# Sixteen heads of attention and a feed-forward: written out in one straight program, or as one loop on the chip with three arms

## The chip, the core and the metric

One Trainium2 core runs the kernel. TensorE (PE) multiplies matrices, VectorE (DVE) does elementwise work and reductions, ScalarE (ACT) activations, GpSimd (POOL) set-up work, and SyncE (SP) issues nearly all DMAs. The metric is the device time of one execution in microseconds, the median of several runs.

## The reference

One decoding step of a transformer block for two sequences. Each of 16 heads reads its whole key and value cache once: 8192 keys of 256 numbers, in float32. That is 8 MB of keys and 8 MB of values for each of the 32 pairs of head and sequence.

```python
B, Sq, D = 2, 1, 448
H, Sk, Dh, F = 16, 8192, 256, 1792
q = (layernorm(x) @ wq).reshape(B, Sq, H, Dh).transpose(0, 2, 1, 3)
scores = einsum("bhqd,bhkd->bhqk", q, k_cache) * (Dh ** -0.5)
o = einsum("bhqk,bhkd->bhqd", softmax(scores), v_cache)
h = x + o.transpose(0, 2, 1, 3).reshape(B, Sq, H * Dh) @ wo
g, u = layernorm(h) @ w_gate, layernorm(h) @ w_up
out = h + (g * u) @ w_down
```

## The kernel before

The program is written out in full: the Python loop `for n in range(NQ + 1)` (L306) leaves no loop on the chip. Step n scores pair n (head n // 2, sequence n % 2) and mixes the values of pair n - 1. A cache of a pair comes in two chunks (c = 0 and 1) of 4 MB, each of which fills one tile `[128, 32, 256]`; four such tiles form a ring, so that k chunk 0, v chunk 0, k chunk 1 and v chunk 1 of successive steps take the same four places again and again.

`scores` (L232) runs on DVE: per pair, four parts of half a chunk, each a multiply of keys by the query (L239) and a reduction (L242). `top` (L246) takes the maximum of a partition on DVE (`m`, L249) and turns the column into a row on PE (`mT`, L251). `softmax` (L253) follows in the next step, after the next pair's first part of scores: `nm` on DVE, a broadcast on PE, the exponential on ACT, the sum on PE (`l_ps`), of which DVE takes the reciprocal (`norm`, L268). `mix` (L272) multiplies probabilities and values on PE, 16 matmuls for a chunk (L278), and `mixed` (L283) sums four strips of the result and, for the second sequence of a head, multiplies by that head's `wo`. Queries are computed for two heads at a time from an 896 KB tile of `wq` (`queries`, L206), and `wo` comes in 448 KB pieces for one head. After the last head comes the feed-forward, with its three weights in the ring's tiles.

The order of the work is that of the code (the schedule is manual): each engine runs its instructions in program order, and waits are derived from who reads and writes a tile. All loads are issued by SP, in the order of the code: k chunk 0, v chunk 0, (a piece of `wo` or `wq`), k chunk 1, v chunk 1. A load into a tile of the ring waits for its last reader: a k load for the DVE multiply L239 of the chunk's second half, a v load for the chunk's PE matmuls L278. What stands behind a waiting load on SP waits too.

Of the kernel before, what the change touches and what calls it, by code (L numbers as in the profile page):

```python
# [24 lines left out]
RING = 4  # L25
WQ, WO = 3 * 2 * DH + DH, 2 * D
# [17 lines left out]
def tile_decode_block(  # L44
# [23 lines left out]
    ring = ctx.enter_context(tc.tile_pool(name="ring", bufs=RING))  # L68
    wpool = ctx.enter_context(tc.tile_pool(name="wpool", bufs=2))
    qpool = ctx.enter_context(tc.tile_pool(name="qpool", bufs=4))  # L70
    work = ctx.enter_context(tc.tile_pool(name="work", bufs=2))
    ps_q = ctx.enter_context(tc.tile_pool(name="ps_q", bufs=2, space=bass.MemoryType.PSUM))
    ps_s = ctx.enter_context(tc.tile_pool(name="ps_s", bufs=2, space=bass.MemoryType.PSUM))
    ps_1 = ctx.enter_context(tc.tile_pool(name="ps_1", bufs=1, space=bass.MemoryType.PSUM))
# [24 lines left out]
    o_ps = [ps_1.tile([P, 2 * DH], F32, name=f"o_ps{i}") for i in range(2)]  # L99
    for t in o_ps:  # L100
        nc.vector.memset(t, 0.0)  # L101
    acc_ps = ps_1.tile([B, D], F32, name="acc_ps")
    y_ps = ps_1.tile([P, YW], F32, name="y_ps")
    nc.vector.memset(y_ps, 0.0)

# [11 lines left out]
    def center(h, tag):  # L117

        mean = ps_s.tile([P, B], F32, tag="sm", name=f"mean_{tag}")
# [18 lines left out]
    def transposed(src, tag):  # L138
        ps = ps_s.tile([P, DC, B], F32, tag="sm", name=f"T_ps_{tag}")
        for c in range(DC):  # L140
            nc.tensor.transpose(ps[:, c, :], src[:, c * P : (c + 1) * P], ident[:B, :B])
        got = const.tile([P, DC, B], F32, name=f"T_{tag}")
        nc.vector.tensor_copy(got, ps)
        return got


    def load_wq(hp):
        t = wpool.tile([P, WQ], F32, tag="wq", name=f"wq_{hp}")
        nc.sync.dma_start(t, wq[hp])
        return t  # L150

    wo_t = {}

    def load_wo(h):

        if h % 2 == 0:
            wo_t[h // 2] = wpool.tile([P, 2, WO], F32, tag="wo", name=f"wo_{h // 2}")
        nc.sync.dma_start(wo_t[h // 2][:, h % 2, :], wo[h])

    def load_cache(src, b, h, c, name, parts=(JC,)):  # L160
        t = ring.tile([P, JC, DH], F32, tag="ring", name=f"{name}_{h}_{b}_{c}")
        n = P * JC
        keys = src[b, h, c * n : (c + 1) * n].rearrange("(p j) d -> p j d", p=P)
        at = 0
        for k in parts:
            nc.sync.dma_start(t[:, at : at + k, :], keys[:, at : at + k, :])
            at += k
        return t

    w_now = load_wq(0)  # L170
# [6 lines left out]
    var = ps_s.tile([P, B], F32, tag="sm", name="var_x")  # L177
# [13 lines left out]
    def first_queries(w):  # L191

        got = [qpool.tile([P, 2, DH], F32, tag="q", name=f"q_0_{b}") for b in range(B)]
        for k in range(2):
            for b in range(B):
                ps = ps_q.tile([P, DH], F32, tag="q", name=f"q_ps_0_{k}_{b}")
                for c in range(DC):
                    at = c * 2 * DH + (k * DH if c < DC - 1 else 0)
                    nc.tensor.matmul(  # L199
                        ps, xb[:, c + (k if c == DC - 1 else 0), b, :], w[:, at : at + DH],  # L200
                        start=(c == 0), stop=(c == DC - 1),
                    )
                nc.scalar.activation(got[b][:, k, :], ps, AF.Copy)
        return got

    def queries(hp, w):  # L206

        got = []
        for b in range(B):
            ps = ps_q.tile([P, 2 * DH], F32, tag="q", name=f"q_ps_{hp}_{b}")  # L210
            for c in range(DC - 1):
                nc.tensor.matmul(  # L212
                    ps, xb[:, c, b, :], w[:, c * 2 * DH : (c + 1) * 2 * DH],
                    start=(c == 0), stop=False,
                )
            for k in range(2):
                nc.tensor.matmul(  # L217
                    ps[:, k * DH : (k + 1) * DH], xb[:, DC - 1 + k, b, :],
                    w[:, 3 * 2 * DH : WQ], start=False, stop=(k == 1),
                )  # L220
            q = qpool.tile([P, 2, DH], F32, tag="q", name=f"q_{hp}_{b}")
            nc.scalar.activation(q.rearrange("p h d -> p (h d)"), ps, AF.Copy)  # L222
            got.append(q)
        return got


    NQ = H * B
    w_t, q_t = {0: w_now}, {0: first_queries(w_now)}
    s_t, p_t, rl_t, l_t, mT_t, oT_t = {}, {}, {}, {}, {}, {}
    HC = JC // 2  # L230

    def scores(i, kt, part):  # L232

        h, b = divmod(i, B)
        if part == 0:
            s_t[i] = work.tile([P, NJ], F32, tag="s", name=f"s_{i}")
        c, k = divmod(part, 2)
        q = q_t[h // 2][b][:, h % 2, :]
        nc.vector.tensor_mul(  # L239
            prod, kt[c][:, k * HC : (k + 1) * HC, :], q[:, None, :].to_broadcast([P, HC, DH])  # L240
        )
        nc.vector.tensor_reduce(  # L242
            s_t[i][:, part * HC : (part + 1) * HC], prod, axis=AX.X, op=ALU.add
        )

    def top(i):  # L246

        m = work.tile([P, 1], F32, tag="m", name=f"m_{i}")
        nc.vector.tensor_reduce(m, s_t[i], axis=AX.X, op=ALU.max)  # L249
        mT_t[i] = ps_s.tile([1, P], F32, tag="sm", name=f"mT_{i}")  # L250
        nc.tensor.transpose(mT_t[i], m, ident)  # L251

    def softmax(i):  # L253
        nm = work.tile([1, 1], F32, tag="nm", name=f"nm_{i}")
        nc.vector.tensor_reduce(nm, mT_t[i], axis=AX.X, op=ALU.max, negate=True)  # L255
        nb_ps = ps_s.tile([P, 1], F32, tag="sm", name=f"nb_ps_{i}")
        nc.tensor.matmul(nb_ps, row, nm, start=True, stop=True)  # L257
        nb = work.tile([P, 1], F32, tag="nb", name=f"nb_{i}")
        nc.scalar.activation(nb, nb_ps, AF.Copy)  # L259
        p_t[i] = work.tile([P, NJ], F32, tag="p", name=f"p_{i}")  # L260
        lsum = work.tile([P, 1], F32, tag="lsum", name=f"lsum_{i}")
        nc.scalar.activation(  # L262
            p_t[i], s_t[i], AF.Exp, bias=nb, scale=DH**-0.5, accum_out=lsum
        )
        l_t[i] = ps_s.tile([P, 1], F32, tag="sm", name=f"l_ps_{i}")
        nc.tensor.matmul(l_t[i], ones, lsum, start=True, stop=True)  # L266

    def norm(i):  # L268
        rl_t[i] = work.tile([P, 1], F32, tag="rl", name=f"rl_{i}")
        nc.vector.reciprocal(rl_t[i], l_t[i])  # L270

    def mix(i, vt, c):  # L272

        o, p = o_ps[i % 2], p_t[i]
# [31 lines left out]
    for n in range(NQ + 1):  # L306
# [15 lines left out]
        if n == NQ:  # L322
            load_wo(H - 1)
# [179 lines left out]
```

## Time and profile before

| | |
|---|---|
| median of 3 runs | 1315.05 us (1314.88 to 1315.12) |
| the profiled execution | 1314.9 us; its span from the first to the last instruction 1313.1 us |
| HBM read | 561.19 MB, 427 GB/s over the span |
| busy | DVE 1153.3 us (88%), PE 569.9 us (43%), ACT 60.7 us (5%) |
| granted TensorE clock | 0.653 (mean) |

The profile is of one execution. A row of its timeline gives start, duration, engine, line and operation, what is written and read, and in brackets how long the engine stood idle before it and what ended that. `SPq` is SyncE issuing a DMA. The DMA queue table gives packets, megabytes and the share of the span that they took of all 16 DMA engines; the kind "instruction" is the engines' own program text being fetched.

### The profile page before, as it was taken

The numbers are of one execution on the slowest core, as the hardware profiler recorded it, in microseconds if no ns is written. First come the engines' busy times: TensorE is split into PE (matmuls) and PEld (weight loads), VectorE is DVE, ScalarE is ACT, GpSimd is POOL, SyncE is SP. The second block draws the span as 40 slices with busy tenths as digits, with TensorE's granted clock in tenths as the row PEclk, the third lists the DMA queues.
The fourth block names the chain that finished last, engine by engine and source line by source line (L and its number), as shares of the span: only waits on it lengthen the run. The fifth ranks groups of instructions, "written<-read, shape, count | busy, mean of one in ns | idle before, by whom it ended". The sixth has DMA issues, their size and how long they took to land.

```text
span 1313.1 us, 6974 instructions
## 1 busy us (share of the span) xinstructions
PE 569.9 (43%) x2936; PEld 173.4 (13%) x2936; DVE 1153.3 (88%) x395; ACT 60.7 (5%) x183; POOL 1.2 (0%) x8
## 2 busy tenths in 40 slices
PE   3224553354432743426433453524525246254357
PEld 2011110111010210102110021101101002011013
DVE  7999999898998899888998889988998989989971
ACT  1000000000000000000000000000000000000000
POOL 0000000000000000000000000000000000000000
PEclk8556766657765666657666567666676667565668
DMA  9999999999999999999999999999999999999997
GB/s 408 430 430 433 430 432 429 428 433 433 431 428 434 430 431 426 435 429 432 431 431 431 434 429 431 430 425 434 430 431 431 433 428 435 431 430 431 431 424 336
DMA packets 23091, 561.64 MB, mean 428 GB/s; under 512 B 2578, under 2 KB 2580, under 8 KB 5908
## 3 DMA queue, kind: packets, MB, share of 16 engines
q1 hardware_dynamic: 23048, 561.20, 99.6%
q8 instruction: 23, 0.38, 0.1%
q14 instruction: 8, 0.07, 0.0%
q10 hardware_dynamic: 12, 0.01, 0.0%
HBM read 561.19 MB, written 0.00 MB: 427 GB/s over the span
## 4 chain that ended last, share of the span: by engine, by line
DMA 79%; PE 14%; DVE 5%; issue 1%; ACT 0%; POOLq 0%; SPq 0%; POOL 0%
DMA v<-in_A_v_cache_dram 77%; PE o_ps L278 13%; DVE prod L239 3%; DMA wu_t<-in_B_w_up_dram 2%; DVE s L242 2%; PE q_ps L199 0%; PE u_ps L379 0%; PE y_ps L438 0%; DVE o_ps L101 0%; PE hm_ps L431 0%; PE oT_ps L291 0%; ACT o_sb L287 0%; PE mean_x L120 0%; DVE xb L134 0%; PE var_x L178 0%
## 5 line engine op out<-in xcount | busy, mean ns | idle before, releaser
L239 DVE TENSOR_TENSOR prod<-k,q 128x4096 f32<-128x4096 f32 x128 | 565.7, 4420 | 115.6 <-DMA k<-in_A_k_cache_dram 110.7
L242 DVE TENSOR_REDUCE s<-prod 128x16 f32<-128x4096 f32 x128 | 565.8, 4420 | 6.0
L278 PE MATMUL o_ps<-v,p 128*2 128x512 f32 x2048 | 371.3, 891 | 338.1 <-DMA v<-in_A_v_cache_dram 338.1
L278 PEld LDWEIGHTS o_ps<-v,p 128*2 128x2 f32 x2048 | 59.2, 109 | 613.6 <-DMA v<-in_A_v_cache_dram 367.3
L257 PE MATMUL nb_ps<-nm,row 1*128 1x1 f32 x64 | 17.9, 347 | 280.0 <-DVE nm L255 280.0
L257 PEld LDWEIGHTS nb_ps<-nm,row 1*128 1x128 f32 x64 | 15.7, 303 | 287.2 <-issue 158.7
L287 ACT ACTIVATE o_sb<-o_ps 128x512 f32<-128x512 f32 x32 | 19.1, 597 | 679.2 <-PE o_ps L278 679.2
L301 PE MATMUL acc_ps<-wo,oT 128*2 128x448 f32 x64 | 43.9, 834 | 5.6 <-ACT oT L297 5.6
L291 PE MATMUL oT_ps<-sel,o_sb 128*128 128x1 f32 x256 | 33.7, 253 | 23.2 <-ACT o_sb L287 23.2
L212 PE MATMUL q_ps<-wq,xb 128*128 128x512 f32 x84 | 39.1, 601 | 0.0
L291 PEld LDWEIGHTS oT_ps<-sel,o_sb 128*128 128x128 f32 x256 | 31.0, 191 | 55.9 <-ACT o_sb L287 55.9
L251 PE MATMUL mT<-ident,m 128*1 128x128 f32 x32 | 10.2, 318 | 61.2 <-DVE m L249 60.9
L266 PE MATMUL l_ps<-lsum,ones 128*128 128x1 f32 x64 | 18.7, 362 | 23.5 <-ACT p L262 23.5
L259 ACT ACTIVATE nb<-nb_ps 128x1 f32<-128x1 f32 x32 | 5.5, 171 | 406.8 <-PE nb_ps L257 406.8
L266 PEld LDWEIGHTS l_ps<-lsum,ones 128*128 128x128 f32 x64 | 16.0, 310 | 26.2 <-ACT p L262 26.2
L212 PEld LDWEIGHTS q_ps<-wq,xb 128*128 128x128 f32 x84 | 15.4, 190 | 20.6 <-issue 20.3
L217 PE MATMUL q_ps<-wq,xb 128*128 128x256 f32 x56 | 14.4, 379 | 0.0
L251 PEld LDWEIGHTS mT<-ident,m 128*1 128x1 f32 x32 | 2.5, 79 | 84.7 <-issue 50.0
L389 DVE TENSOR_TENSOR h_sb<-x_sb,acc_ps 2x448 f32<-2x448 f32 x1 | 0.6, 609 | 13.8 <-PE acc_ps L301 13.8
L222 ACT ACTIVATE q<-q_ps 128x512 f32<-128x512 f32 x14 | 8.4, 597 | 92.1 <-PE q_ps L217 92.1
L217 PEld LDWEIGHTS q_ps<-wq,xb 128*128 128x128 f32 x56 | 10.6, 190 | 7.4 <-issue 6.7
L262 ACT ACTIVATE p<-s,nb 128x64 f32<-128x64 f32 x32 | 11.1, 348 | 1.0
(79 smaller groups left out, 101.8 us busy)
## 6 DMA issues: line engine op xcount, KB each, us to landing
k<-in_A_k_cache_dram SPq DMA_DIRECT2D x63, 4096.0 KB, 26.5
v<-in_A_v_cache_dram SPq DMA_DIRECT2D x63, 4096.0 KB, 33.2
wq<-in_wq_dram SPq DMA_DIRECT2D x8, 896.0 KB, 34.6
wo<-in_wo_dram SPq DMA_DIRECT2D x16, 448.0 KB, 33.5
k<-in_A_k_cache_dram SPq DMA_DIRECT2D x2, 2048.0 KB, 13.5
wg_t<-in_B_w_gate_dram SPq DMA_DIRECT2D x1, 3136.0 KB, 24.5
wu_t<-in_B_w_up_dram SPq DMA_DIRECT2D x1, 3136.0 KB, 30.4
v<-in_A_v_cache_dram SPq DMA_DIRECT2D x1, 2048.0 KB
```

The costliest lines, as they stand in the source:

```text
L212: nc.tensor.matmul(ps, xb[:, c, b, :], w[:, c * 2 * DH : (c + 1) * 2 * DH], start=(c == 0), stop=False,)
L217: nc.tensor.matmul(ps[:, k * DH : (k + 1) * DH], xb[:, DC - 1 + k, b, :], w[:, 3 * 2 * DH : WQ], start=False, stop=(k == 1),)
L239: nc.vector.tensor_mul(prod, kt[c][:, k * HC : (k + 1) * HC, :], q[:, None, :].to_broadcast([P, HC, DH]))
L242: nc.vector.tensor_reduce(s_t[i][:, part * HC : (part + 1) * HC], prod, axis=AX.X, op=ALU.add)
L251: nc.tensor.transpose(mT_t[i], m, ident)
L257: nc.tensor.matmul(nb_ps, row, nm, start=True, stop=True)
L262: nc.scalar.activation(p_t[i], s_t[i], AF.Exp, bias=nb, scale=DH**-0.5, accum_out=lsum)
L266: nc.tensor.matmul(l_t[i], ones, lsum, start=True, stop=True)
L278: nc.tensor.matmul(o[g : g + 2, :], p[:, 2 * t : 2 * t + 2], vt[c][:, j : j + 2, :], start=(t < 4), stop=(t >= NJ // 2 - 4),)
L287: nc.scalar.activation(o_sb, o_ps[i % 2], AF.Copy)
L291: nc.tensor.matmul(oT_ps[:, c : c + 1], o_sb[:, (2 * k + c) * P : (2 * k + c + 1) * P], sel[:, k : k + 1], start=(k == 0), stop=(k == 1),)
L301: nc.tensor.matmul(acc_ps, oT_t[h][:, c, :], w[:, c * D : (c + 1) * D], start=(h == 0 and c == 0), stop=(h == H - 1 and c == 1),)
```

## The change

The heads become one loop on the chip, `tc.For_i(0, H, 1, iteration_sync="reg_based")`, of 16 turns. A turn does both sequences of a head, and holds three arms behind two branches: turn 0 (no values to mix for its first pair), turn 15 (with the last pair's mix and the feed-forward), and the rest. All tiles are fixed now: `k_sb[0..1]` and `v_sb[0..1]` in place of the ring of four, one `wq_sb` and one `wo_sb` of 448 KB, one of each small tile but queries, scores and probabilities, of which there is one for each sequence. `wq` is loaded and used for one head in each turn, in place of two heads in every second. Addresses of loads come from registers that are worked out from the turn. Ahead of the loop SP issues the first `wq`, both key chunks of pair 0 (into `k_sb[1]` and `v_sb[1]`), the first key chunk of pair 1 and the first value chunk of pair 0: 16 MB. The residual `x` is put into `acc_ps` by a matmul before the loop, and is not added after it. The feed-forward's arithmetic is unchanged.

```diff
-    for n in range(NQ + 1):
-        kt, vt = [], []
...
-            if n < NQ:
-                parts = FIRST if n == 0 and c == 0 else (JC,)
-                kt.append(load_cache(k_cache, n % B, n // B, c, "k", parts))
-            if n > 0:
-                parts = LAST if n == NQ and c == NCH - 1 else (JC,)
-                vt.append(load_cache(v_cache, (n - 1) % B, (n - 1) // B, c, "v", parts))
...
+    def query_steps(h, first, more):
+        for b in range(B):
+            before = b > 0 or not first
+            for c in range(NCH):
+                if not first or (b > 0 and c > 0):
+                    load_cache(k_sb[c], k_cache, b * H + h, c)
+                    load_cache(v_sb[c], v_cache, h if b else H - 1 + h, c)
+                if c == 0 and b == 0 and before:
+                    load_w(wo_sb, wo, h)
+                if c == 0 and b == 1 and more:
+                    load_w(wq_sb, wq, h)
+            at = k_sb if before else k_first
+            scores(b, 0, at)
+            if before:
+                softmax(1 - b)
+            scores(b, 1, at)
+            if before:
+                norm()
+            for part in range(2, 2 * NCH):
+                scores(b, part, at)
+            for c in range(NCH):
+                if c > 0 and b == 1 and more:
+                    query(0)
+                    query(1)
+                    take_query(0)
+                if before:
+                    mix(1 - b, c)
+            if before:
+                mixed(1 - b)
+            top(b)
+            if b == 1 and more:
+                take_query(1)
...
+    k_first = (k_sb[1], v_sb[1])
+    for c in range(NCH):
+        load_cache(k_first[c], k_cache, 0, c, FIRST if c == 0 else (JC,))
+    load_cache(k_sb[0], k_cache, H, 0)
+    load_cache(v_sb[0], v_cache, 0, 0)
+    with tc.For_i(0, H, 1, name="heads", iteration_sync="reg_based", hint_engines=()) as i:
+        with tc.If(i == 0) as at_first:
...
+            query_steps(0, True, True)
+        with at_first.Else():
+            with tc.If(i == H - 1) as at_last:
+                query_steps(H - 1, False, False)
+                attend_last()
+                feed_forward()
+            with at_last.Else():
+                query_steps(i, False, True)
```

The order of the cache loads is the same as before; the weights stand elsewhere between them (`wo` one pair later, `wq` in each turn's second pair). What a load waits for has changed. SyncE's loads of one head in the program before (head 2; the name is tile, sequence or head, chunk; each counter in brackets is an engine's or a DMA's):

```order
L166 DMA k_2_0_0_435<-in_A_k_cache_dram 128x8192 [waits DMAHW7_49,DMAHW4_49,DVE_49]
L166 DMA v_1_1_0_437<-in_A_v_cache_dram 128x8192 [waits DMAHW0_49,PE_49]
L166 DMA k_2_0_1_439<-in_A_k_cache_dram 128x8192 [waits DMAHW2_49,DVE_49]
L166 DMA v_1_1_1_441<-in_A_v_cache_dram 128x8192 [waits DMAHW3_49,PE_49]
L166 DMA k_2_1_0_511<-in_A_k_cache_dram 128x8192 [waits DMAHW4_49,DVE_49]
L166 DMA v_2_0_0_513<-in_A_v_cache_dram 128x8192 [waits DMAHW5_49,DMAHW1_49,PE_49]
```

and the start of the arm of the rest, now, on the same engine (the counters named `I-151_own` are the loop's own, and an `ISA` row works out registers):

```order
L170 ISA [waits DMAHW0_I-151_own]
L170 DMA k_sb0_94<-in_A_k_cache_dram 128x8192 [waits DMAHW0_I-151_own,DMAHW5_I-151_own,DVE_I-151_own,DMAHW6_I-151_own,PE_I-151_own,DMAHW5_49]
L170 ISA [waits DMAHW1_I-151_own]
L170 DMA v_sb0_96<-in_A_v_cache_dram 128x8192 [waits DMAHW1_I-151_own,DMAHW2_I-151_own,PE_I-151_own,DMAHW6_49]
L174 ISA [waits DMAHW2_I-151_own]
L174 DMA wo_sb_99<-in_wo_dram 128x896
```

The waits of the two loads moved. In the loop a wait is for a count that must mean the same whichever arm the turn before took. Added up through the built program, each turn raises PE's counter by 238 in every arm, and the first `v_sb[0]` load of turn t waits for 238 times t + 1: 476 in turn 1, 714 in turn 2. PE reaches that count with the last instruction of the turn before. The first `k_sb[0]` load waits for DMA counters that stand for the last `k_sb[1]` load of the turn before, and the `ISA` row ahead of the `v_sb[0]` load for that turn's last `v_sb[1]` load. The other loads of a turn wait for the readers that they waited for before. What PE's last instruction of a turn is, shows the end of that arm:

```order
L251 MATMUL o_ps0_83<-v_sb1_97,p_sb0_104 2x512 [waits DMAHW1_I-151_own]
L251 MATMUL o_ps0_83<-v_sb1_97,p_sb0_104 2x512 x15
L262 ISA
L262 MATMUL sm_ps1_93<-sel_81,o_sb_111 128x1 [waits DVE_I-151_own,Activation_I-151_own]
L262 MATMUL sm_ps1_93<-sel_81,o_sb_111 128x1 x3
L231 REGISTER_ALU
L231 MATMUL sm_ps0_92<-ident_65,m_sb_106 1x128 [waits DVE_I-151_own]
L436 UNCONDITIONAL_BRANCH
L429 ISA
```

and the same place in the program before, between two heads on PE:

```order
L291 MATMUL oT_ps_1_331<-sel_99,o_sb_1_329 128x1 [waits Activation_49]
L291 MATMUL oT_ps_1_331<-sel_99,o_sb_1_329 128x1 x3
L301 MATMUL acc_ps_105<-wo_0_192,oT_0_259 2x448 [waits DMAHW7_49,Activation_49]
L301 MATMUL acc_ps_105<-wo_0_192,oT_0_259 2x448
L251 MATMUL mT_2_341<-ident_83,m_2_339 1x128 [waits DVE_49]
L257 MATMUL nb_ps_2_357<-nm_2_355,row_92 128x1 [waits DVE_49]
```

The transpose of the maxima (L231 now, L251 before) has kept its place on PE; but it is now the last instruction of a turn, it comes after DVE's maximum over the pair's last scores, and it is what raises the counter to the value that the next turn's first v load waits for. Behind it PE takes two branches and continues.

More of the change, by code (lines that the diff above doesn't have):

```diff
@@ L206, in queries @@
[L206 to L224, printed above, removed]
@@ L244, in scores, with top @@
         )
[L246 to L261, printed above, removed]
+    def top(b):
+        nc.vector.tensor_reduce(m_sb, s_sb[b], axis=AX.X, op=ALU.max)
+        nc.tensor.transpose(sm_ps[0][:1, :P], m_sb, ident)
```

375 lines of the change are left out of this document (176 added, 199 removed).

## The prediction

> **What bounds the kernel now.** I read the page's busy times and DMA table first, then what SyncE waits for, then the timeline of one head, then the start and the end.
>
> ```profile
> PE 569.9 (43%) x2936; PEld 173.4 (13%) x2936; DVE 1153.3 (88%) x395; ACT 60.7 (5%) x183; POOL 1.2 (0%) x8
> ...
> DMA packets 23091, 561.64 MB, mean 428 GB/s; under 512 B 2578, under 2 KB 2580, under 8 KB 5908
> ...
> q1 hardware_dynamic: 23048, 561.20, 99.6%
> q8 instruction: 23, 0.38, 0.1%
> q14 instruction: 8, 0.07, 0.0%
> ```
>
> The 16 DMA engines are busy for 99.6% of the span: the caches' bytes are the bound, and no engine's work is. A change can gain only what little of the stream is not data; it can lose wherever it lets the stream run dry. The two instruction rows are program text: 23 fetches by one queue of 0.38 MB (16 KB each), 8 smaller ones by another.
>
> ```profile
> SPq L166 <- DVE prod L239: 858.3, 63, 17.6
> ...
> SPq L166 <- PE o_ps L278: 148.5, 59, 3.8
> ```
>
> SyncE waits nearly all the time: for DVE's multiply before it may refill a k tile, and for PE's mix before a v tile. That costs nothing while loads are queued, which the timeline shows:
>
> ```profile
> 690.50 0.33 SPq L166 DMA_DIRECT2D k<-in_A_k_cache_dram  x1
> ...
> 693.92 0.33 SPq L166 DMA_DIRECT2D v<-in_A_v_cache_dram  x1
> ...
> 697.55 4.42 DVE L239 TENSOR_TENSOR prod<-k,q 128x4096 f32<-128x4096 f32 x1 [2.55 <-DMA k<-in_A_k_cache_dram]
> ...
> 707.22 6.46 PE L278 MATMUL o_ps<-v,p 128*2 128x512 f32 x32 [13.37 <-DMA v<-in_A_v_cache_dram]
> 710.91 0.33 SPq L166 DMA_DIRECT2D k<-in_A_k_cache_dram  x1
> ...
> 713.75 0.33 SPq L166 DMA_DIRECT2D v<-in_A_v_cache_dram  x1
> ...
> 714.41 1.05 PE L291 MATMUL oT_ps<-sel,o_sb 128*128 128x1 f32 x8 [0.73 <-ACT o_sb L287]
> 715.38 0.22 DVE L249 TENSOR_REDUCE m<-s 128x1 f32<-128x64 f32 x1
> ...
> 715.65 0.27 PE L251 MATMUL mT<-ident,m 128*1 128x128 f32 x1 [0.19 <-DVE m L249]
> 716.92 4.43 DVE L239 TENSOR_TENSOR prod<-k,q 128x4096 f32<-128x4096 f32 x1 [1.32 <-DMA k<-in_A_k_cache_dram]
> ...
> 738.58 4.43 DVE L239 TENSOR_TENSOR prod<-k,q 128x4096 f32<-128x4096 f32 x1 [3.67 <-DMA k<-in_A_k_cache_dram]
> ```
>
> A pair's k chunk 1 is there at 697.55, the next pair's k chunk 0 at 716.92, with the v chunk 1 between them: 19.4 us for two chunks, 9.7 us each. From 716.92 to 738.58, 21.7 us, lie a v chunk, an 896 KB `wq` and a k chunk; `wq` is 2.2 us, 448 KB 1.1. The k and v loads that SyncE issued at 690.50 and 693.92 refill tiles for pieces that land after 707: some 15 to 20 us of lead. DVE needs 18.05 us from 697.55 to the end of `m` at 715.60.
>
> **The change part by part.** *The wait at a turn's start.* The first `v_sb[0]` load of a turn now waits for PE's last instruction of the turn before, the transpose of `m`, where before it waited for a mix that was over long since (the load issued at 693.92 is of that kind, 22 us ahead of the `mT` at 715.65). With the rows above, and 697.55 as the moment when a turn's last k chunk is there: the transpose ends at 715.65 + 0.27 = 715.92, SyncE answers 0.07 us later (713.68, the end of the mix at 707.22, to 713.75) and passes one more register wait, about 0.1: issue at 716.1. Queued ahead of it then is only the rest of k chunk 0, which lands at 716.9. So the stream restarts from nothing. What a restart costs, the start of the program tells:
>
> ```profile
> 0.73 0.39 SPq L149 DMA_DIRECT2D wq<-in_wq_dram  x1
> ...
> 1.19 2.35 SPq L166 DMA_DIRECT2D k<-in_A_k_cache_dram  x4
> ```
> ```profile
> DMA to landing us min/median/max: 13.5/18.1/22.7
> ```
> ```profile
> GB/s 0 0 0 0 0 0 0 0 0 0 0 0 0 0 0 0 36 430 287 72 215 215 0 502 287 358 430 287 215 860 72 215 932 72 215 860 143 645 358 143
> ```
>
> The second row is of the k loads issued between 1.3 and 2.2 us; the quickest, the second half of the first chunk, is issued at 1.19 + 0.41 = 1.60 and lands 13.5 us later, at 15.1. By then 896 + 2048 + 2048 KB are through, 11.8 us at 9.7 for 4096. Issue at 0.73 to landing at 15.1 is 14.4, so a cold start costs 2.5 us. The strip (the first 4 us in 40 slices) has the first packets 1.0 us after the issue; that is the lower end. The v chunk then lands at 716.1 + 9.7 + 2.5 = 728.3, against 716.9 + 9.7 = 726.6: late by 1.7 us, or by 0.2 with 1.0. I take 1.4, near the upper end, since that one is measured from issue to landing and the strip shows a ramp behind the first packet. It returns in each of turns 2 to 15, since DVE then waits for k again at the turn's end: 14 x 1.4 = 19.6 us.
>
> *Turn 1 costs more*, since DVE starts late and runs behind the stream until 137 us:
>
> ```profile
> 78.96 28.30 DMA v<-in_A_v_cache_dram
> 107.30 6.10 PE o_ps L278 x32
> ```
> ```profile
> 83.00 0.22 DVE L249 TENSOR_REDUCE m<-s 128x1 f32<-128x64 f32 x1
> ...
> 83.28 0.37 PE L251 MATMUL mT<-ident,m 128*1 128x128 f32 x1 [13.04 <-DVE m L249]
> ```
> ```profile
> 137.62 4.43 DVE L239 TENSOR_TENSOR prod<-k,q 128x4096 f32<-128x4096 f32 x1 [0.59 <-DMA k<-in_A_k_cache_dram]
> ```
>
> Pair 1's v chunk 1 landed at 107.26; its v chunk 0, two chunks and a `wq` earlier, at 107.26 - 19.4 - 2.2 = 85.7, and in the new order, with 448 KB less ahead of it, it would at 84.6. But it is issued only after the `mT` that ends at 83.65: 83.8 + 2.5 + 9.7 = 96.0, or 94.5 with the lower restart. Late by 11.4 us (9.9 to 11.4). DVE has caught up after that.
>
> *Program text.* Before, it is read straight through. One fetch of 16 KB holds up one DMA engine, and the slowest engine sets when a load has landed:
>
> ```profile
> 515.71 4.43 DVE L239 TENSOR_TENSOR prod<-k,q 128x4096 f32<-128x4096 f32 x1 [1.38 <-DMA k<-in_A_k_cache_dram]
> ...
> 536.27 4.42 DVE L239 TENSOR_TENSOR prod<-k,q 128x4096 f32<-128x4096 f32 x1 [2.56 <-DMA k<-in_A_k_cache_dram]
> ...
> 557.05 4.42 DVE L239 TENSOR_TENSOR prod<-k,q 128x4096 f32<-128x4096 f32 x1 [2.74 <-DMA k<-in_A_k_cache_dram]
> ```
> ```profile
> q8 instruction: 1, 0.02, 2.3%
> ```
>
> From 536.27 to 557.05 is 20.8 us in place of 19.4 for two chunks, and the second answer is of 549 to 552 us, with one fetch in it: 1.4 us. Where fetches fall on different DMA engines in turn, most cost nothing, since the others run ahead meanwhile. In the loop they can't: the stream empties once a turn, all engines start together, and any fetch between that start and the turn's last k chunk delays the turn by 1.4 us. PE is the engine with much text (2936 matmuls and as many loads fill the 23 fetches); a middle turn needs some 400 of its instructions, behind two jumps over the text of two other arms. If those blocks are read anew each turn: 14 x 1.4 = 19.6 us. If not, 0. I take them as read anew, since nothing in the trace shows text being used twice; the fetch steps at 557 and at one or two other places (about 2.8 us) then fall away from the old account. [...]
>
> *The branches themselves*: all engines jump at a turn's end. DVE is free at 715.60 and needs k at 716.92; a stall of a few us is made up in the same turn. I cost it at 0, covered by the waits for k (1.3 and 3.7 us in the rows at 716.92 and 738.58, as much again in the turn's other half, and the lateness that the v load brings). PE is next wanted after DVE's first half chunk, 9 us on. Register work ahead of waits runs while the engine is busy: 0.
>
> *Weights*: `wq` per head is the same bytes in all: 0. PE's extra matmuls lie beside 57% idle time: 0.
>
> *The end.*
>
> ```profile
> 1309.94 0.28 DVE y L444
> ```
> ```profile
> SPq L487 <- PEq L487: 0.7, 1, 0.7
> ```
>
> The tail keeps its order and its loads; `x` is added by a matmul before the loop instead of on DVE. At the exit comes one barrier more, 0.7 us by the one at the start.
>
> The sum on the span: 1313.1 + 11.4 + 19.6 + 19.6 - 2.8 + 0.7 = 1361.6. The profiled execution took 1314.9, and the median is 1315.05, 1.95 above the span: **1363.5 us**.
>
> **The rivals.** *Text costs nothing*: PE keeps its blocks, or their fetch falls into the 1 to 2 us in which the stream is empty anyway, right after the jump. For it: the jump comes at 715.9, just then. Against it: there is more than one block, and the later ones come when data flows. Then 1363.5 - 19.6 = 1344 us.
>
> *The other side: the gate does not close.* If the count that SyncE waits for is reached with the mix, as before (in the rows, 713.68 minus a turn's worth of lead), the stream never empties and the loop's shorter text leaves the three fetch steps out: 1315.05 + 0.7 - 4.2 = 1311.5. It decides if the v load is issued more than 2.5 us ahead of the landing of k chunk 0, that is before 714.4. Against it stands the `mT`: in the row it starts at 715.65, after `m`, and the count is not complete before it.
>
> *Jumps stall the engines for long.* DVE can begin 6 us late after `m` and still be in time for k chunk 1, and gain 3.7 more in the turn's two other gaps; beyond some 9.8 us each one costs 14. With 12 us: 1363.5 + 14 x 2.2 = 1394. For it: three jumps in a row; against it: DVE's text is 395 instructions in all, small.
>
> **How the numbers follow.** The forecast 55%, text for nothing 30%, long stalls 10%, no gate 5%. The forecast's own range, with a turn's lateness at 0.7 to 1.7 us and text at 0.8 to 1.7, is 1345 to 1372; the text-free case with the same lateness reaches from 1334 to 1348, and to 1327 with the lowest lateness, 0.2, which I hold unlikely. From 1336 to 1385 leaves out the gate that does not close, most of the long stalls and the lowest edge of the text-free case. Under 0.2% (2.6 us) a measurement can't tell a change here; faster by more has 4%, within it 2%, slower 94%.
>
> **What would show it.** Right: SyncE's longest total wait at L170 is for PE at L231, 15 times; in each turn one v load is issued just after an `mT`, and the DMA strip has a dip once in 80 us, the widest near 84 us; DVE's waits for k grow by 2 to 4 us a turn; instruction fetches number over 60 in place of 31, and a turn takes 82 to 83 us. Wrong: as many fetches as before or fewer (then text costs nothing), turns of 79.9 us (then no gate), or DVE idle ahead of the first L221 of a turn for 10 us without a DMA ending it (then long stalls). A count that PE reaches with another instruction than L231 would make the prediction wrong at its root.

## The result, and the profile after

The loop takes 1355.39 us (median of 6 runs, 1353.08 to 1356.33) against 1315.09 before (6 runs, 1314.88 to 1315.52): 1.0302 times as long, 95% interval 1.0288 to 1.0315. The forecast was 1363.5, its range 1336 to 1385. The profiled execution has a span of 1353.6 us against 1313.1, 40.5 more.

The page of the kernel after, busy times, GB/s by slice of 33.8 us, and DMA queues:

```profile
PE 552.1 (41%) x3094; PEld 193.6 (14%) x3094; DVE 1153.7 (85%) x395; ACT 61.5 (5%) x197; POOL 1.2 (0%) x8
...
GB/s 407 401 268 432 409 412 430 393 421 413 432 432 413 432 406 432 432 412 432 406 434 415 428 431 407 432 412 432 431 409 432 411 430 426 416 432 404 431 429 336
...
q1 hardware_dynamic: 24200, 561.20, 97.3%
q8 instruction: 13, 0.21, 0.1%
q14 instruction: 4, 0.03, 0.0%
```

No engine has more to do than before. The DMA engines moved the same 561.20 MB, but were busy for 97.3% of the span in place of 99.6%. The strip is full (428 or more) in about half its slices and holds one deep dip, 268, from 68 to 102 us, and shallow ones near 410 where a turn starts. And there are fewer fetches of program text than before, 13 + 4 in place of 23 + 8, not more.

What SyncE waited for (total us, times, longest):

```profile
SPq L170 <- DVE prod L221: 421.1, 33, 17.2
...
SPq L170 <- PE sm_ps L231: 142.5, 15, 22.2
```

and its queue, with DVE and PE, at the start of a turn:

```profile
724.45 0.33 SPq L170 DMA_DIRECT2D k_sb<-in_A_k_cache_dram  x1
...
741.91 0.22 DVE L230 TENSOR_REDUCE m_sb<-s_sb 128x1 f32<-128x64 f32 x1
...
742.19 0.27 PE L231 MATMUL sm_ps<-ident,m_sb 128*1 128x128 f32 x1 [1.49 <-DVE m_sb L230]
742.59 0.33 SPq L170 DMA_DIRECT2D v_sb<-in_A_v_cache_dram  x1
743.19 0.33 SPq L174 DMA_DIRECT2D wo_sb<-in_wo_dram  x1
743.64 4.42 DVE L221 TENSOR_TENSOR prod<-k_sb,q_sb 128x4096 f32<-128x4096 f32 x1 [1.50 <-DMA k_sb<-in_A_k_cache_dram]
744.03 0.33 SPq L170 DMA_DIRECT2D k_sb<-in_A_k_cache_dram  x1
744.78 0.33 SPq L170 DMA_DIRECT2D v_sb<-in_A_v_cache_dram  x1
```

This is the gate. Between 724.45 and 742.59 SyncE issues nothing; it stands at the v load until PE has done L231, then issues four loads in 2.2 us. DVE's start at 743.64 says when k chunk 0, the last load in the queue, had landed: the v load was issued less than 1 us ahead of that. Before, the load of this kind had 23 us (issued at 693.92, with k chunk 0 there at 716.92).

DVE pays for it in waits (total us, times, longest; there was only a row like the first before, 110.7 us in 57 waits; in the second SyncE, at L494, passes on to the loop's own counters that a k chunk has landed, at 724.02 for a landing at 723.99):

```profile
DVE prod L221 <- DMA k_sb<-in_A_k_cache_dram: 110.7, 46, 6.1
DVE prod L221 <- SPq L494: 34.3, 13, 2.7
```

Landing times in the DMA records of the trace give the account (a 4 MB load in a full stream lands 9.71 us after the one ahead; "late" is what is above that):

| where | late, us | the forecast's term |
|---|---|---|
| pair 2's k chunk 0, waiting for DVE, which starts at 13.66 in place of 11.51 | 3.2 | none |
| turn 1's v load, some 1.6 of it text fetches (below) | 12.4 | 11.4 |
| turn 2's v load, some 1.8 of it text fetches | 3.5 | 1.4 |
| the v loads of turns 3 to 15, 1.47 to 1.74 each | 21.7 | 13 x 1.4 = 18.2 |
| a text fetch before the last arm (the load that lands at 1285.8) | 1.4 | 14 x 1.4 = 19.6 |
| three fetch steps of before, gone | -4.3 | -2.8 |
| last landing to the end of the span, 5.1 in place of 3.8 | 1.3 | 0.7 |
| sum | 39.2 of 40.5 | 48.5 |

Turns 1 and 2 hold more than the gate. In turns 3 to 15 the first of the 16 DMA engines lands the gated load 11.6 to 11.8 us after its issue, the last 12.0 to 12.3. In turns 1 and 2 the first takes as long (11.7 and 11.8), but the last takes 13.8 and 14.0, and fetches of text lie there (16 KB each, at 86.7, 92.8 and 94.2, and at 173.8 and 175.0). In turn 2 the load is issued 0.81 us ahead of the landing of k chunk 0, as later (0.71 to 0.83): DVE had caught up. Of the 3.2 us of the first row, too, about 1 is on the last engine alone, with a fetch at 63.7.

### The profile page after: what moved, and what is told of

Same layout as the page of the kernel before. It is cut to its first block, busy times and chain, and to the rows that moved or that the text cites. A ratio compares the mean times of both kernels' runs of the same rounds, so it can differ in the third digit from the quotient of the medians.

```text
span 1353.6 us, 9219 instructions
## 1 busy us (share of the span) xinstructions
PE 552.1 (41%) x3094; PEld 193.6 (14%) x3094; DVE 1153.7 (85%) x395; ACT 61.5 (5%) x197; POOL 1.2 (0%) x8
## 3 DMA queue, kind: packets, MB, share of 16 engines
q1 hardware_dynamic: 24200, 561.20, 97.3%
## 5 line engine op out<-in xcount | busy, mean ns | idle before, releaser
L221 DVE TENSOR_TENSOR prod<-k_sb,q_sb 128x4096 f32<-128x4096 f32 x126 | 556.9, 4420 | 153.2 <-DMA k_sb<-in_A_k_cache_dram 110.7
L224 DVE TENSOR_REDUCE s_sb<-prod 128x16 f32<-128x4096 f32 x128 | 565.7, 4420 | 5.4
L251 PE MATMUL o_ps<-v_sb,p_sb 128*2 128x512 f32 x2048 | 359.3, 865 | 379.2 <-DMA v_sb<-in_A_v_cache_dram 250.5
L251 PEld LDWEIGHTS o_ps<-v_sb,p_sb 128*2 128x2 f32 x2048 | 58.5, 107 | 639.0 <-DMA v_sb<-in_A_v_cache_dram 262.5
L236 PE MATMUL sm_ps<-nm_sb,row 1*128 1x1 f32 x64 | 18.2, 350 | 293.4 <-DVE nm_sb L234 293.4
L205 PE MATMUL q_ps<-wq_sb,xb 128*128 128x256 f32 x192 | 50.0, 397 | 0.0
L262 PE MATMUL sm_ps<-sel,o_sb 128*128 128x1 f32 x256 | 33.7, 253 | 25.7 <-ACT o_sb L258 25.7
L262 PEld LDWEIGHTS sm_ps<-sel,o_sb 128*128 128x128 f32 x256 | 31.0, 191 | 56.5 <-ACT o_sb L258 56.5
L205 PEld LDWEIGHTS q_ps<-wq_sb,xb 128*128 128x128 f32 x192 | 35.0, 196 | 18.5 <-issue 14.9
L269 PE MATMUL acc_ps<-wo_sb,oT_sb 128*2 128x448 f32 x64 | 34.4, 671 | 5.6 <-ACT oT_sb L266 5.6
L231 PE MATMUL sm_ps<-ident,m_sb 128*1 128x128 f32 x32 | 10.0, 314 | 58.6 <-DVE m_sb L230 58.5
L210 PEld LDWEIGHTS q_ps<-wq_sb,xb 128*128 128x128 f32 x128 | 19.8, 196 | 1.8
L210 PE MATMUL q_ps<-wq_sb,xb 128*128 128x128 f32 x128 | 19.9, 279 | 0.0
L231 PEld LDWEIGHTS sm_ps<-ident,m_sb 128*1 128x1 f32 x32 | 2.5, 79 | 75.9 <-issue 51.0
## 6 DMA issues: line engine op xcount, KB each, us to landing
k_sb<-in_A_k_cache_dram SPq DMA_DIRECT2D x2, 2048.0 KB, 11.4
v_sb<-in_A_k_cache_dram SPq DMA_DIRECT2D x1, 4096.0 KB, 22.2
```

Of the source, the lines that this page charges most:

```text
L205: nc.tensor.matmul(q_ps[b][:, :DH], xb[:, c, b, :], wq_sb[:, c * DH : (c + 1) * DH], start=(c == 0), stop=False,)
L210: nc.tensor.matmul(q_ps[b][:, k * HD : (k + 1) * HD], xb[:, DC - 1 + k, b, :], wq_sb[:, 3 * DH :], start=False, stop=(k == 1),)
L221: nc.vector.tensor_mul(prod, at[c][:, k * HC : (k + 1) * HC, :], q_sb[b][:, None, :].to_broadcast([P, HC, DH]))
L224: nc.vector.tensor_reduce(s_sb[b][:, part * HC : (part + 1) * HC], prod, axis=AX.X, op=ALU.add)
L231: nc.tensor.transpose(sm_ps[0][:1, :P], m_sb, ident)
L236: nc.tensor.matmul(nb_ps, row, nm_sb, start=True, stop=True)
```

## The experiments

Two theories stood at the start. **A**, the gate: a load that is issued too late lets the stream run dry, and a restart is the price. **B**, the loop itself: jumps, registers ahead of each DMA, fixed tiles, engines that start a turn together. The times of the kernel before in the shared runs were 1315.05 to 1315.12 us throughout.

**The transpose moved (e1).**

```diff
     def top(b):
         nc.vector.tensor_reduce(m_sb, s_sb[b], axis=AX.X, op=ALU.max)
-        nc.tensor.transpose(sm_ps[0][:1, :P], m_sb, ident)
     def softmax(b):
+        nc.tensor.transpose(sm_ps[0][:1, :P], m_sb, ident)
```

> The loop as it is, but PE's transpose of the maxima (L231) stands at the start of softmax, in the next pair, and not at the end of a turn; nothing else moves. PE's last instruction of a turn is then the sum of strips (L262), which needs only the mix. Theory A, the gate: the time comes from the v load that waits for L231. Then the late landings of the gated v loads go (12.4 us in turn 1, 3.5 in turn 2, 13 x 1.67 in the rest = 37.6 us of the trace of the loop): 1355.4 - 37.6 = 1317.8 us, between 1313 and 1321; the waits of SyncE at L170 for L231 are gone from the rows, turns take 79.9 us. Theory B, the loop itself (jumps, registers ahead of DMAs, engines that start a turn together, fixed tiles): the time stays at 1345 to 1356, turns at 81.6 us.

Measured: 1337.64 us (1336.0 to 1341.5), ratio 1.0178 [1.0164, 1.0192]; neither. The start of a turn in its timeline:

```profile
400.17 1.05 PE L262 MATMUL sm_ps<-sel,o_sb 128*128 128x1 f32 x8 [0.81 <-ACT o_sb L258]
...
401.35 0.33 SPq L170 DMA_DIRECT2D v_sb<-in_A_v_cache_dram  x1
...
403.33 4.43 DVE L221 TENSOR_TENSOR prod<-k_sb,q_sb 128x4096 f32<-128x4096 f32 x1 [1.51 <-DMA k_sb<-in_A_k_cache_dram]
```

The gate is not gone, it has moved: the v load still waits for PE's last instruction of the turn, now the sums L262, because the count stands for the whole turn. My expectation took the end of the mix for what the load waited for before; that was the mix of chunk 0, a chunk earlier. The load now has 1.8 us of lead in place of 0.8, and lands 0.85 us late here in place of 1.7; over the run the late landings at turn starts add up to some 23 us, and the run is 22.5 slower than before. So the late landings are the price, which speaks for A. Here, and at 482.71 and 889.25, the lead counts us for us. In eleven turns it is 2.5 to 2.7 us: two of these loads land on time, nine 0.7 to 2.7 us late, though their first engine lands 11.6 to 11.9 us after the issue as in the loop. Only one of the nine has text fetches close to it, so why their last engine lags stays open.

**The gate alone in the straight program, first try (e2, e6).**

```diff
         if n < NQ:
             top(n)
+            if n % 2 == 1:      # e6: if n > 0
+                nc.tensor.matmul(y_ps[0:1, 0:1], vt[0][:, 0, 0:1], ones[:, 0:1], start=True, stop=True)
```

> The straight program of before, with the gate alone: behind every second pair's transpose of maxima PE runs one small matmul that reads the tile into which the next first v load goes, so that this load waits for the maxima as in the loop, 15 times. No loop, no jump, no register. Theory A, the gate: 1315.1 + 37.6 = 1352.7 us, between 1345 and 1357, with 16 rows of PE waits of SyncE as long as in the loop. Theory B, the loop itself: 1315 to 1318, since 15 matmuls of 0.3 us lie beside PE's idle time.

> As the run with the gate in the straight program, but behind the maxima of every pair: the cost doubled, 30 gates. Theory A, with each gate costing one restart of an empty stream: 15 more gates x 1.67 us = 25 us over that run, 1378 us, between 1370 and 1386. If instead the cost of a gate came from DVE being behind, it would be the same lateness spread over more gates and the time would stay within 8 us of that run. Theory B: 1315 to 1320.

Measured: 1321.43 us [1.0035, 1.0062] and 1321.67 us [1.0036, 1.0063]. That looks like B, but the timeline of e2 shows that the wait sat on another load:

```profile
798.52 0.33 SPq L166 DMA_DIRECT2D v<-in_A_v_cache_dram  x1
801.12 0.33 SPq L166 DMA_DIRECT2D k<-in_A_k_cache_dram  x1
...
803.45 0.19 PE L345 MATMUL y_ps<-ones,v 128*1 128x1 f32 x2
803.67 0.33 SPq L166 DMA_DIRECT2D v<-in_A_v_cache_dram  x1
804.59 4.43 DVE L239 TENSOR_TENSOR prod<-k,q 128x4096 f32<-128x4096 f32 x1 [1.39 <-DMA k<-in_A_k_cache_dram]
```

The pool gave the tile that the small matmul kept busy to v chunk 1, and when that was issued at 803.67 two loads, 8 MB, were queued ahead (798.52 and 801.12). A late issue with that much ahead of it cost nothing that the two runs show: 15 or 30 such gates, the same time within 0.3 us. Most of the 6 us that both are slower is one load of the start: the v load issued at 78.54 (78.66 in e6), behind a queue that had been empty since 75.8, lands 5.2 us late (5.5).

**The gate on the right load (e7, e8).** The same edits, and four fixed tiles in place of the pool:

```diff
-    ring = ctx.enter_context(tc.tile_pool(name="ring", bufs=RING))
+    tiles, taken = [const.tile([P, JC, DH], F32, name=f"ring{i}") for i in range(RING)], []
+    def next_tile():
+        taken.append(tiles[len(taken) % RING])
+        return taken[-1]
```

> The straight program again with the gate alone, now on the right load: the pool that hands out the four tiles is replaced by four fixed tiles in turn, as in the loop, so that the small matmul behind every second pair's transpose of maxima holds back v chunk 0 of the next pair and, on SyncE's queue, both chunks behind it. (With the pool, the tile that the matmul kept busy was handed to v chunk 1, with 8 MB queued ahead of it, and two k chunks went where v chunks had been.) Theory A, sharpened: a load into an empty stream lands 2.6 us later than in a full one (issued at 416.14, landed 428.42: 12.28 against 9.71), so a gate costs 2.6 us less the lead that its issue has over the landing of the load ahead (1.0 us in the loop, 1.7 in the run with the transpose moved). Here the maxima come as in the loop: 12 to 13 us at the first gate, 3.5 at the second, 13 x 1.67 at the rest: 1352.7, between 1345 and 1358. Theory B, the loop's boundary costs the time (jumps, registers, all engines in step): 1315 to 1322, as with the pool.

> The same with fixed tiles, a gate at every pair: 30 in place of 15. Theory A: 15 more x 1.6 to 1.7 us = 25 us over the run with 15: 1378, between 1368 and 1386. Theory B: within 4 us of the run with 15 gates, at 1315 to 1324.

Measured: 1368.93 us, ratio 1.0409 [1.0395, 1.0423], and 1421.81 us, ratio 1.0789 [1.0762, 1.0815]. Without any loop the gate alone costs 54 us: B is not needed. (The fixed tiles, the other change here, are in e14 too, which costs 1 us.) It costs more than the loop that it was taken from, and that is the second finding. In e7's waits and DMA table:

```profile
SPq L171 <- PE y_ps L350: 405.3, 16, 26.6
```
```profile
q8 instruction: 23, 0.38, 0.1%
```

Its 16 gated loads land late by 10.5 us at first and 1.6 to 2.3 then, 36.5 in all, as in the loop. Another 18.6 us are 16 loads that land 0.5 to 1.6 us late (mostly 1.1 to 1.5) some 7 to 9 us behind a fetch of text (fetches at 513, 639, 701, 763; late landings at 522, 646, 708, 772). This is the prediction's mechanism: the gate lets all 16 DMA engines start level (the first and the last land 15 of the 16 gated loads 0.4 to 0.7 us apart), and then a fetch on one of them holds up the load. Without gates they are not level (the first engine of a load lands up to 5.6 us before the last, in the kernel before) and most fetches hide in that (23 fetches there, three late steps). In the loop fetches do this in turns 1 and 2 and at the last arm; between 230 and 1277 us none comes.

e7 lies above A's range (1345 to 1358) by that text, which the expectation left out. e8 missed in size: 53 us more for 15 more gates, not 25. At a dozen of them PE is late, since the product with `wo` stands ahead of the transpose:

```profile
993.62 0.22 DVE L254 TENSOR_REDUCE m<-s 128x1 f32<-128x64 f32 x1
...
994.16 2.49 PE L306 MATMUL acc_ps<-wo,oT 128*2 128x448 f32 x4 [0.35 <-ACT oT L302]
...
995.13 4.43 DVE L244 TENSOR_TENSOR prod<-ring,q 128x4096 f32<-128x4096 f32 x1 [1.29 <-DMA ring<-in_A_k_cache_dram]
...
996.57 0.37 PE L256 MATMUL mT<-ident,m 128*1 128x128 f32 x1
...
997.10 0.33 SPq L171 DMA_DIRECT2D ring<-in_A_v_cache_dram  x1
```

The load ahead had landed (995.11) when the gated one was issued, and it is 4.4 us late.

**The next loads issued early (e9, e10).** The next turn's first k and v load stand at the end of the turn's own arm, where their readers are known one by one:

```diff
             if b == 1 and more:
                 take_query(1)
+                load_cache(k_sb[0], k_cache, h + 1, 0)
+                load_cache(v_sb[0], v_cache, H + h, 0)
```

and the arms leave them out at their start. In e10 the other six cache loads of a turn are split into halves, `(HC, HC)`, besides.

> The loop with the next turn's k chunk 0 and v chunk 0 issued at the end of the turn's own arm, where the true readers are known: the wait for PE's last instruction is gone. A turn still has 10 loads on 8 counters, so its last two loads share counters with the next turn's first two, and these wait until they have landed: the next k chunk 1 is issued only when v chunk 0 has landed. Theory A (an empty stream costs 2.6 us less the lead, whatever empties it): lead 0, so 15 x 2.6 = 39 us over the loop without a gate (1317.8): 1357, between 1350 and 1362, no better than the loop. If only the gate on PE mattered, 1318; by theory B (the loop itself) 1335 to 1345, as with the transpose moved.

> As the run with the next loads issued early, but six of a turn's cache loads are split into two halves of 2 MB, so that a turn has 16 loads and each counter is used again only after 8 loads, as in the straight program. Nothing waits for more than its true reader or a load long landed. Theory A: 1317.8, between 1313 and 1322, with no landing later than 0.5 us but at the start and at the fetches of text. Theory B, the loop itself costs: 1335 or more.

Measured: 1345.01 us, ratio 1.0226 [1.0212, 1.024], and 1324.43 us, ratio 1.0071 [1.0057, 1.0084]. In e9 SyncE's queue at a turn's start is:

```profile
405.97 0.33 SPq L174 DMA_DIRECT2D wo_sb<-in_wo_dram  x1
415.79 0.33 SPq L170 DMA_DIRECT2D k_sb<-in_A_k_cache_dram  x1
416.54 0.33 SPq L170 DMA_DIRECT2D v_sb<-in_A_v_cache_dram  x1
```

By the time alone this would be B's range (1335 to 1345), and A's 1357 was missed. But PE's gate is gone and another closes, as A said: k chunk 1, issued at 415.79, waits until v chunk 0 has landed (415.35), since they share a counter. It did not cost 2.6 but mostly 1.7 to 1.9 us a turn, because `wo`, issued at 405.97, was still queued behind v chunk 0 and landed at 416.45. e10 is 2.4 us above A's range. It has no landing over 0.5 us late after 100 us but for two, of 0.6, with text fetches near the end. So what is above 1317.8 is not lateness. Its halves take 4.89 us (median of 187 landings) against 9.71 for a whole load, 0.08 more for every 4 MB, 92 times: 7 to 8 of the 9 us that it is slower than the straight program.

One rule sizes most of these restarts. Issue and landings are of one gated load each, from the DMA records:

| kernel | issued | load ahead landed | landed | late by | late + lead |
|---|---|---|---|---|---|
| loop | 416.14 | 416.98 | 428.42 | 1.73 | 2.57 |
| e1 | 401.35 | 403.11 | 413.67 | 0.85 | 2.61 |
| e9 | 415.79 | 416.45 | 427.86 | 1.70 | 2.36 |
| e8 | 997.10 | 995.11 | 1009.24 | 4.42 | 2.43 |

Where no fetch of text lies behind the gate, nearly all the gated loads of the loop from turn 3 on, of e7, e8 and e9 come to 2.3 to 2.7 us like these. So in these runs a load had to be issued some 2.5 us before the last one ahead of it landed, and what was missing of that was lost. It is a floor and no guarantee: nine loads of e1 had that lead and came late all the same.

**Whole cache loads, weights in pieces (e11, e12).** e11 is e9 with each weight load cut into four of 32 rows; e12 adds the start of before.

> As the run with 16 loads a turn, but the six extra loads come from the weights (each in four pieces of 32 rows, 112 KB) and not from the caches, which are whole again. In the run before, a cache load of 2 MB took 4.90 us where half of 4 MB is 4.86 (medians 4.90 and 9.71), 0.08 us more for each 4 MB split, some 90 of them: 7 us of its 9. Theory C, the price hangs on the halves of caches: it goes with whole ones, and the time is 1316 to 1318. Theory D, the price is one of each further DMA, whatever its size: the same six more DMAs a turn, 1323 to 1325. Theory B (the loop itself costs the rest): 1324 too.

> As the run with the weights in four, and with the start of before: x is transposed by PE's transpose and not by matmuls, and the matmul that puts x into the sum comes behind the first queries. Theory: DVE's first multiply starts some 1 to 2 us sooner (13.66 in the loop, 11.51 before), and the lateness of the first k_sb[0] load (2.3 us in the run with 16 loads, at 76) goes with it: 1 to 2 us less than the run with the weights in four; 1314 to 1316. If the start is hidden: no difference, within 0.5 us.

Measured: 1427.23 us (1411.92 to 1442.72), ratio 1.0851 [1.0819, 1.0884], and 1418.03 us (1410.97 to 1430.44), ratio 1.0781 [1.0747, 1.0815]. Both theories on the halves fell short of what happened, and the runs scatter too much to say anything of the start. In e11's DMA records the first of 16 engines lands the cache load ahead of each group of pieces on time, the last 2.3 to 3.1 us late; over three loads a group costs some 3 us, 31 times, which is nearly all of the 97 us that the profiled execution lost (span 1410.0). Why pieces of 32 rows do that stays open.

**Longer arms (e5, e13).** Four heads and two heads in a turn:

```diff
-    with tc.For_i(0, H, 1, name="heads", ...) as i:
+    with tc.For_i(0, H, 2, name="heads", ...) as i:      # e5: 4
...
                 query_steps(i, False, True)
+                query_steps(i + 1, False, True)          # e5: up to i + 3
```

> The loop with four heads in each turn: 4 turns, 3 gates in place of 15, and a middle arm with some 1650 matmuls of PE in place of some 410. Theory A, and text that stays: the first gate comes when DVE has caught up, so 3 x 1.67 = 5 us: 1317.8 + 5 = 1323, between 1318 and 1328, and few fetches (the arms' text once, some 23 to 30 packets of text in all). If text is read anew in each turn once an arm is longer than what stays: fetches in the second middle turn too, a step of 1.4 us for each stretch of them, 1326 to 1340. Theory B, a cost by turn of (1355.4 - 1315.1) / 15 = 2.7 us: 1315.1 + 3 x 2.7 = 1323, so this run does not tell B from A; it is for the text.

> The loop as it was put in, with two heads in each turn: 8 turns, 7 gates, and a middle arm of some 825 matmuls of PE in place of some 410 (four heads, 1650 matmuls, read their text anew each turn: 41 packets for PE and 10 to 17 us at a boundary). Text that stays: gates alone, the first with DVE still some 5 us behind, the others 1.7 each: 1317.8 + 5 + 6 x 1.7 = 1333, between 1328 and 1338, with fetches in the first two turns only. Text read anew: fetches of PE in every turn and boundaries that cost 4 to 10 us: 1340 to 1375.

Measured: 1350.17 us, ratio 1.0275 [1.0261, 1.0289], and 1358.41 us, ratio 1.0328 [1.0315, 1.0342]: with a fifth of the gates 5 us faster than the loop, with half of them 3 us slower. e5 lies above its range even for text read anew (1326 to 1340), e13 inside the one for it (1340 to 1375). (The expectations count some 410, 825 and 1650 matmuls of PE in an arm; the traces show 178, 356 and 712, and as many weight loads.) DMA queues of e5, then of e13:

```profile
q8 instruction: 41, 0.67, 0.2%
q14 instruction: 61, 0.50, 0.1%
```
```profile
q8 instruction: 40, 0.66, 0.2%
q14 instruction: 42, 0.34, 0.1%
```

Here text is read anew after the first turns too, and it is not PE alone that waits for it. The start of a turn in e13, with the wait of DVE and its total:

```profile
821.77 0.22 DVE L230 TENSOR_REDUCE m_sb<-s_sb 128x1 f32<-128x64 f32 x1
822.45 0.33 SPq L170 DMA_DIRECT2D v_sb<-in_A_v_cache_dram  x1
...
837.18 4.43 DVE L221 TENSOR_TENSOR prod<-k_sb,q_sb 128x4096 f32<-128x4096 f32 x1 [15.19 <-issue]
```
```profile
DVE prod L221 <- issue: 106.8, 7, 23.2
```

No DMA of data ends that gap ("issue"): k chunk 0 landed at 823.30. DVE's sequencer takes jumps here, and three times it goes on 1.8 to 1.9 us after a fetch of 8 KB: fetches at 823.0, 829.3 and 835.0, its next steps at 824.86, 831.05 and 836.90. Then DVE begins. DVE waits so at the start of each of e13's seven later turns (gaps of 9.3 to 23.2 us). In e5 the longest such gap is 30.4 us, and the loads around that turn's start are late by some 17 us together. This is the rival of long stalls, in arms that are twice and four times as long.

PE's text does not follow the same rule. Its last jump at the start of a turn (L437; duration in ns, start), in the third and the fifth of these seven turns, and all the text that was fetched from 800 to 1150 us:

```profile
L437 PEldq COMPARE_BRANCH  x1: 8033/8033/8033, 502.9 to 502.9; - x1
```
```profile
L437 PEldq COMPARE_BRANCH  x1: 200/200/200, 822.8 to 822.8; - x1
```
```profile
q14 instruction: 10, 0.08, 0.1%
```

PE's jump waits where 16 KB fetches of q8 come, so q8 is taken for PE's queue. They come at the start of the first four turns of the seven; at the start of the last three none does, PE's jumps take some 0.2 us, and DVE's gap at 837.18 is 15 us as before. Why PE reads the arm anew four times and then keeps it stays open. In e5 it is read anew in all of its three.

**No gate, whole loads (e14).**

```diff
                     load_cache(k_sb[c], k_cache, b * H + h, c)
+                    if b == 0:
+                        load_w(wo_sb, wo, h)
                     load_cache(v_sb[c], v_cache, h if b else H - 1 + h, c)
...
         with tc.If(i == 0) as at_first:
+            for n in range(5):
+                nc.sync.dma_start(const.tile([1, P], F32, name=f"pad{n}"), wo[0, n : n + 1, :P])
```

with the early loads of e9 and the start of e12.

> The loop with the next turn's k chunk 0 and v chunk 0 issued in the turn's own arm, all caches in whole loads, ten loads a turn, and no wait that empties the stream: wo stands behind k chunk 1, so that what shares a counter with the two early loads is a k chunk 1 (waits for k chunk 0, with v chunk 0 still to come) and wo (waits for v chunk 0, with k chunk 1 still to come); the first arm starts with five loads of 512 bytes into tiles that nobody reads, so that each load has the same counter in every arm. The start is that of before (PE's transpose of x, the matmul of x behind the first queries). Theory A: without an empty stream the loop costs what the straight program costs but for its exit (+1.3 us) and a start and text as before: 1315 to 1317, turns of 79.9 us, no landing later than 0.5 us in turns 3 to 14. Theory B', splitting the caches was not what cost 9 us in the run with 16 loads, the loop is: 1322 to 1325, cache loads of 4 MB at 9.8 us.

Measured: 1316.12 us (11 runs, 1315.51 to 1316.87), ratio 1.0007 [0.9998, 1.0016]: as theory A had it (1315 to 1317), and no difference from the straight program that can be told. Its GB/s strip, text fetches and a turn's start:

```profile
GB/s 411 411 425 432 432 426 429 431 433 432 429 431 433 432 431 431 433 429 431 432 433 431 431 434 429 431 431 432 433 430 433 433 426 433 430 433 430 432 423 325
...
q8 instruction: 13, 0.21, 0.1%
```
```profile
396.05 0.22 DVE L230 TENSOR_REDUCE m_sb<-s_sb 128x1 f32<-128x64 f32 x1
...
397.88 4.43 DVE L221 TENSOR_TENSOR prod<-k_sb,q_sb 128x4096 f32<-128x4096 f32 x1 [1.61 <-SPq L499]
398.04 0.33 SPq L173 DMA_DIRECT2D k_sb<-in_A_k_cache_dram  x1
...
407.59 0.33 SPq L177 DMA_DIRECT2D wo_sb<-in_wo_dram  x1
408.34 0.33 SPq L173 DMA_DIRECT2D v_sb<-in_A_v_cache_dram  x1
```

What is issued at a turn's start now has a whole load ahead of it: k chunk 1 at 398.04 has v chunk 0, `wo` and v chunk 1 at 407.6 and 408.3 have k chunk 1. The strip is flat. Jumps, registers and fixed tiles are all still there, so B is out: with the gate opened the loop costs 1.0 us, about its longer exit. And of the 9 us of e10, 8 went when its loads were whole again (the earlier start of DVE, 12.42 in place of 13.66, may hold a little of it). No version here beats the straight program by what can be measured.

## Why the prediction was right, and where it was not

*The wait at a turn's start* was right in place, number and cause: 15 waits for L231, a v load right behind it in every turn, DVE's waits for k longer by 34.3 us, 2.3 a turn, as forecast (2 to 4). Undersized: 1.67 us a turn in place of 1.4. The forecast had worked out 1.7 from the start of the program, issue to landing, and went below it for the sake of the first packet's 1.0; the measured restart, 2.3 to 2.6 us in the loop, is the first figure (2.5).

*Turn 1*: 12.4 for 11.4, but some 1.6 of it are text; the wait alone is 10.8, inside the 9.9 to 11.4 of the prediction. And there are 3.2 more that no term held. The start of the kernel was costed at nothing, but DVE began 2.15 us later: PE turns `x` by eight passes of matmul (1.83 us) in place of four transposes, which end at 3.2. *Turn 2*: "DVE has caught up after that" held, by the lead of 0.81 us; of its 3.5 us some 1.7 are the gate and 1.8 text.

*Program text* is the step that failed. Put at 19.6 us, it cost some 5 to 6: in turns 1 and 2, at the last arm, and about 1 us ahead of turn 1. The mechanism of the term was there, a fetch behind a gate that holds up one engine's share of the load (in turn 1 the last engine lands it 13.8 us after the issue, in turns 3 to 15 12.0 to 12.3); that it returns in every turn was the forecast's estimate, and wrong: no run shows the 14 x 1.4 us. After 229 us PE fetches nothing until the last arm, at 1277.8; the loop has 13 fetches where it should have had many more, and the old steps are gone, 4.3 us (the sum had 2.8, the rival without a gate 4.2 for the same three). "Nothing in the trace shows text being used twice" was true of the trace and no reason, since a straight program can't show it. The sign of it given in the prediction, fewer fetches than before, is what came. How much text can stay is shown in part: in its last turns e13's PE goes through 759 instructions at a turn without a fetch, by estimate 47 KiB at the 64 bytes each that 23 fetches of 16 KB for 5918 instructions come to in the kernel before; e5's arm of 1508 instructions, some 94 KiB by the same estimate, was read anew in each of its three turns. Where between the two PE's text stops staying is not shown.

So the time came out within 8 us of the forecast in part by luck: text, some 14 us too high, stood beside terms that were some 6 us too low together, 1.3 of which no landing accounts for. The range held because it covered both text cases. The rival *text costs nothing* was nearer in the mechanism; its 1344 is 11 too low for the text that did come and the same undersized terms. *The gate does not close* was ruled out by L231's 15 waits; *long stalls* by DVE's 1.50 us ahead of 743.64, which a DMA ended. The turn of 82 to 83 us was 81.6 (issues at 416.14 and, four turns on, 742.59). That the longest total wait at L170 would be for L231 was wrong: DVE's 421.1 is longer.

The *other edits at nothing* hold for branches, register work, weights and PE's extra matmuls: e14 keeps them all and costs 1 us. *The exit* took 1.3, not 0.7.

## What to carry to other kernels

In a loop with arms, look for what each wait of a turn's first loads stands for: here it stood for a whole turn of PE (15 waits for L231, up to 22.2 us), and the cure was to issue those loads at the end of the arm that knows their readers, with each load at the same place in every arm's sequence (e14, 1316.12 us). A late issue was priced here by its lead over the landing of what was queued ahead, at least 2.3 to 2.7 us less the lead, and by nothing at all with 8 MB ahead (e2 and e6, 1321.43 and 1321.67 us); a lead of just 2.6 us was not safe in e1 (nine of eleven such loads came 0.7 to 2.7 us late). Keep an arm short enough that its text stays, on every engine: two heads in a turn halved the gates here and cost as much again (e13, 1358.41 us against 1355.39).

## What the chip did that I had not expected

- The one-head arm (178 matmuls and as many weight loads on PE) was read in turns 1 and 2 and then no more. Of the two-head arm (356) PE's text was read in four turns and then no more, DVE's in all seven. What decides this is not shown.
- Where its text is fetched anew at a jump, DVE stood still for 9 to 30 us, with small fetches some 6 us apart while loads were streaming (823.0, 829.3 and 835.0 in e13). PE's jumps waited some 8 us where its text was fetched (8.0 at 502.9 in e13, 7.8 at 170.04 in the loop) and 0.2 where it was not; but DVE's gap was the same 15 us with PE's text there, so PE's much larger text did not set the pace.
- A text fetch cost 0.5 to 1.6 us behind a gate and mostly nothing in a long stream (16 such steps in e7, three in the kernel before, with 23 fetches of PE's size in each).
- 2 MB loads took 4.89 us where 4 MB took 9.71, and four pieces of 32 rows in place of one weight load cost some 3 us a group.
